# Tile 5's transposition moved from TensorE to memory moves and VectorE, in a fused linear-attention and MLP kernel

## The chip, the core and the metric

The kernel runs on one core of a Trainium2 chip. The core has a matrix engine (TensorE, "PE"; its weight loads are listed apart as "PEld"), VectorE ("DVE"), ScalarE ("ACT"), GpSimd ("POOL") and SyncE ("SP", which here issues nearly all DMAs). The engines run their own instruction streams in order and wait for each other through semaphores; DMA transfers run on 16 DMA engines of the core. The metric is the device time of one execution in microseconds (us). The kernel before took 416.17 us (median of three runs, 414.56 to 416.19).

## What is computed

An input `x` of 2048 tokens by 512 features is layer-normalised (no learned scale), and the result `xn` goes into two branches that are added to `x`:

```
xn  = (x - mean(x)) / sqrt(var(x) + 1e-5)
q, k, v = xn @ wqkv                    # 32 heads of 16
pq, pk  = phi(q), phi(k)               # phi(t) = t + 1 if t > 0 else exp(t), plus 1e-6
A   = (pq @ (pk^T v)) / (pq . sum(pk)) # per head
B   = relu(xn @ w1 + b1)^2 @ w2 + b2   # 1376 hidden units
out = x + A @ wo + B
```

All inputs and outputs are float32.

## The kernel before

The 2048 tokens are 16 tiles of 128 tokens. Products are made in a reduced float32 format on PE, in three passes of a high and a low part (`h` and `l`): high x high, high x low, low x high. So each operand is first split: the high part is a rounding copy (ACT mostly), the low part the difference (DVE or POOL).

The first part of the program, about the first 100 us, is the one that matters here. It goes over the 16 tiles, normalises each, brings it in two layouts and forms the key side of the attention:

- `xp[i]` is the normalised tile with tokens on partitions. Split by `tokens(i)` (L349: high on ACT, low on POOL) it is one operand of `kx(i)`.
- The same tile with features on partitions ("turned") is split into the column slots of `xsb` (`xs0` or `xs1`, chosen by `cols(i)`): `high` on ACT (L325), `low` on DVE (L328). `project(i, ...)` (L367, twelve matmuls) multiplies it with the key weights into a PSUM bank `pk{i}`. The first eight matmuls need the high part, the last four the low part.
- `phi_k` (L380) makes `phi` of it: two activations on ACT (L361, L363), one instruction on DVE (L365, tile `k`). `parts(i)` (L373) splits that: high on ACT (L377), low on DVE (L378, tile `pk`).
- `kx(i)` (L384, twelve matmuls) adds the products of tile i's tokens and its `pk` to four PSUM banks.

The loop at L779 runs i from 2 to 15. Its pass i issues, in this order: the memory moves that are due (`move()`, L784), `project(i)`, the transposes of a later tile, `phi_k(i)`, the normalisation of a later group (`normalise(*soon)`), `parts(i)`, the token split of tile i + 1, the turn of tile i + 2 (L831, where that is done by DVE), statistics of a later tile, in passes 3 and 6 two stores of 1 MB each (`xsd`, L843 to 845), and last `kx(i - 1)`. The order of the program is the order on each engine, since the schedule is written by hand.

There are two ways to turn a tile.

- Tiles below `NDVE` (6 before the change, so tiles 0 to 5): `turned_pe` (L304) has four PE transposes against an identity (L309) into a PSUM bank; `high` and `low` read that bank, and `keep_t` copies it with ACT to SBUF so that SP can store it to `xTd` for later use (L337). Tiles 3, 4 and 5 are turned so in passes 2, 3 and 4, between `project(i)` and `kx(i - 1)` on PE.
- The other tiles go in pairs: `regroup` (L278) stores the pair of normalised tiles to a DRAM buffer `via` with one DMA (L282) and notes four moves that bring it back regrouped by blocks of 32 partitions into `xg` (L290). `move()` issues noted moves at the head of the next pass. Each move waits until the `via` store has landed. `turn` (L292, L294) is then one DVE instruction that transposes 32x32 blocks. No PE and no PSUM bank is used. For such tiles `xp[i]` is stored with its features regrouped.

Tiles 6 and 7 are the only ones below `NPE` = 8 that go the second way. Tiles below 8 are normalised by DVE (L269), later ones by ACT (L259).

Statistics (L230, L231) are gathered in groups that share two small activations and three small DVE instructions. The groups before the change:

```
soon = group(4, 6, 7)         # L628; measured before the loop, normalised in pass 2
if i == 2:                    # L834
    ahead[3] = statistics(5)  # normalised in pass 3
```

Tiles 8 and 9, 10 and 11, and so on follow in pairs (`ahead[4]`, `ahead[6]`, ...), normalised in passes 4, 6, 8 and 10. The pairs' moves are issued in passes 5, 7, 9 and 11, and their first tile is turned at the end of passes 6 and 8, then, from pass 11 on, in front of `phi_k`. The pair 6 and 7 is normalised in pass 2, moved at the head of pass 3 and turned at the end of passes 4 and 5.

In pass 3, before the moves, SP also loads the bias `b1` with four small DMAs (L780 to 783); it is first used after 100 us.

After the loop come the attention matrices and two rounds of the MLP and query products; the change doesn't touch them.

Of the kernel before, what the change touches and what calls it, by code (L numbers as in the profile page):

```python
# [7 lines left out]
F32 = mybir.dt.float32  # L8
# [5 lines left out]
P = 128  # L14
# [4 lines left out]
def kernel(  # L19
# [36 lines left out]
    NJ = D // P  # L56
    TB = 4
# [1 line left out]
    BT = TB * P  # L59
    NF = -(-F // P)  # L60
    NPE = 2 * TB
    NDVE = NPE - 2
    WARM = 11
    NP = NF // 2
    FP = NF * P
# [7 lines left out]
    work = ctx.enter_context(tc.tile_pool(name="work", bufs=1))  # L73
# [4 lines left out]
    def bank(name, tag="ps"):  # L78
        return psum.tile([P, 512], F32, name=name, tag=tag)

    def w512(name, tag, bufs):
        return work.tile([P, 512], F32, name=name, tag=tag, bufs=bufs)
# [8 lines left out]
    def two(name):  # L91
        return keep.tile([P, 2, 512], F32, name=name, tag=next_tag("x"))

    def four(name, tag, dt=F32, pool=None):
        return (pool or work).tile([P, TB, 512], dt, name=name, tag=tag)
# [7 lines left out]
    def gjc(ap):  # L103

        return ap.rearrange("p (j g c) -> p g j c", j=NJ, g=NJ)
# [11 lines left out]
    def split(h, l, src, eh, el):  # L117
        copy(eh, h, src)
        ENG[el].tensor_tensor(out=l, in0=src, in1=f32(h), op=OP.subtract)  # L119
# [35 lines left out]
    xr, xp, xg, tok, pk, kp = {}, {}, {}, {}, {}, {}  # L155
# [17 lines left out]
    def units(f):  # L173


        if f < NF - 1:
            return [(0, f * P, P)]
        return [(0, f * P + Q, 2 * Q), (2 * Q, f * P, Q), (3 * Q, f * P, Q)]
# [44 lines left out]
    def group(*tiles):  # L223
        return tiles, *(small.tile([P, 3, k], F32, name=f"{n}{tiles[0]}", tag=n) for n, k in (("st", 6), ("mv", 2), ("y", 3)))

    def measure(g, *ks):

        tiles, st, mv, _ = g
        for k in ks or range(len(tiles)):
            nc.vector.bn_stats(st[:, k, :], xr[tiles[k]])  # L230
            nc.vector.bn_aggr(mv[:, k, :], st[:, k, :])  # L231

    def statistics(*tiles):
        g = group(*tiles)
        measure(g)
        return g

    def roots(tiles, st, mv, y):

        n = len(tiles)  # L240
        nc.scalar.activation(y[:, 1, :n], mv[:, :n, 1], AF.Ln, bias=eps)
        nc.scalar.activation(y[:, 0, :n], y[:, 1, :n], AF.Exp, scale=-0.5)

    def normalise(tiles, st, mv, y):
# [18 lines left out]
        for k, i in enumerate(tiles):  # L263
            o, src = xp[i], xr[i]
            if i >= NDVE:

# [20 lines left out]
    def move(n=8):  # L287
        for _ in range(n):
            if moves:
                nc.sync.dma_start(*moves.pop(0))  # L290
# [6 lines left out]
    def slot(i):  # L297
        return slice((i % TB) * P, (i % TB + 1) * P)
# [5 lines left out]
    def turned_pe(i, n=1):  # L304

        t = [bank(f"pt{i}{k}", "acc" if i < 3 else "ps")[:, :D // n] for k in range(n)]
        for j in range(NJ):
            k, at = divmod(j * P, D // n)
            nc.tensor.transpose(t[k][:, at:at + P], xp[i][:, j * P:(j + 1) * P], ident)  # L309
        ones(i)  # L310
        return [p.rearrange("p (j t) -> p j t", j=NJ // n) for p in t]

    def transposed(i, n=1):

        b, at = i // TB, slot(i)
        if i < NDVE:
            t = turned_pe(i, n)
# [12 lines left out]
        def keep_t():  # L330
            o = t[0]
            if i < NDVE:
                o = w512(f"t{i}", "p", 6).rearrange("p (j t) -> p j t", j=NJ)
# [11 lines left out]
    def ones(i):  # L345

        nc.gpsimd.memset(xp[i][:, D - 1:] if i < NDVE else xp[i][:, NJ - 1, P - 1:], 1.0)

    def tokens(i):  # L349
        tok[i] = pair(f"tok{i}")  # L350
        h, l = tok[i][:, 0], tok[i][:, 1]
        src = xp[i]
        if i >= NDVE:
            h, l, src = gjc(h), gjc(l), src.rearrange("p g (j c) -> p g j c", j=NJ)
        split(h, l, src, "act", "pool")
        if NDVE <= i + 1 < NT:
            ones(i + 1)
# [9 lines left out]
    def project(i, ps, w, steps, first=True, last=True):  # L367

        for n, (j, u, v) in enumerate(steps):
            nc.tensor.matmul(ps, lhsT=cols(i)[u][:, j, slot(i)], rhs=w[v][:, j, :], start=first and n == 0,  # L370
                             stop=last and n == len(steps) - 1)

    def parts(i):  # L373

        p = kp[i]
        pk[i] = pair(f"pk{i}")
        copy("act", pk[i][:, 0], p, 1e-6)  # L377
        nc.vector.scalar_tensor_tensor(pk[i][:, 1], p, 1e-6, f32(pk[i][:, 0]), op0=OP.add, op1=OP.subtract)  # L378

    def phi_k(i, ps, mid=lambda: None, late=lambda: None):  # L380
        kp[i] = w512(f"k{i}", "p", 6)
        phi(ps, kp[i], mid, late)
# [139 lines left out]
    t, rk = two("x0"), four("rk", "r0")  # L522
# [17 lines left out]
    groups = {}  # L540
    x4, x8 = four("x4", "r1"), four("x8", "r2")
    for i0 in range(0, NT, TB):
        a = first_xp[i0]
        for k in range(TB):
            xp[i0 + k] = a[:, k]
        if i0 + TB <= NDVE:
            continue
        n = TB if i0 >= NPE else NPE - NDVE
        o = work.tile([P, n, 512], F32, name=f"xg{i0}", tag="r0" if i0 + TB == NT else "r3" if i0 >= NPE else "rc")
        for k in range(0, n, 2):  # L550
            i = i0 + TB - n + k
            u, v = (t.rearrange("p a (g c) -> p (a g c)", g=NJ) for t in (a[:, TB - n + k:][:, :2], o[:, k:k + 2]))
            groups[i + 1] = [t.rearrange("p (g n) -> p g n", g=NJ) for t in (u, v)]
            u, v = (t.rearrange("p (g i c) -> p g i c", g=NJ, i=2) for t in (u, v))
            for m in range(2):
                xp[i + m], xg[i + m] = u[:, :, m], v[:, :, m]
# [68 lines left out]
    load_x(12, two("x12"))  # L625
    load_x(14, two("x14"))
    project(2, pks[2], wk, HL)
    soon = group(4, 6, 7)  # L628
    phi_k(0, pks[0])
    measure(soon, 0)  # L630
    tokens(0)
# [5 lines left out]
    measure(soon, 1)  # L637
    tokens(1)
    parts(1)
    measure(soon, 2)  # L640


    def tokens_sum(n, tag):
        return keep.tile([P, 2, 2, 512], F32R, name=f"T{n}", tag=tag)
# [32 lines left out]
    def fetch():  # L677
        while todo and len(held) < 3:
            held.append(todo.pop(0)())
# [89 lines left out]
    def more(i=None):  # L769

        if i is None or i > 12:
            do(extra, counts[0].pop(0))


    ahead = {}
# [1 line left out]
    kxp = [bank(f"kx{c}", "acc") for c in range(NJ)]  # L777
    kx(0)
    for i in range(2, NT):  # L779
        if i == 3:  # L780
            nc.sync.dma_start(b1s[:, :NF - 1], b1[:(NF - 1) * P].rearrange("(f p) -> p f", p=P))
            for a, o, n in units(NF - 1):
                nc.sync.dma_start(b1s[a:a + n, NF - 1:], b1[o:o + n, None])
        move()  # L784
        fetch()
        ps = pks[i] if i < 3 else bank(f"pk{i}")
        if i > 2:
            project(i, ps, wk, HL)
        high = low = keep_t = lambda: None
        if i + 1 < NDVE:  # L790
            high, low, keep_t = transposed(i + 1)

        soon_turned = transposed(i + 2) if 11 <= i and i + 2 < NT else ()

        def mid():
            high()
            more(i)

        def late():
            if soon:  # L800
                roots(*soon)
            low()
            more(i)

        if i == 12:
            rawz = raw_1(NF - 1)
            T.update({n: tokens_sum(n, f"B{n - 1}") for n in (1, 2)})
        if i == 12:
            w = load_1("q", 0)
        if i == 13:  # L810
            todo_1 = operands_first(0, w)
            extra.append(todo_1.pop(1))
        if i == 14:
            z = pair("w1z0")
            extra.append(lambda: split(z[:, 0], z[:, 1], rawz, "act", "dve"))
            o34 = halves(four("Tf", "r0"))
            extra.extend(sums_of(xT[NB - 1], xT[NB - 2], *o34))
            lows = [extra.pop() for k in range(2)]
            extra += [todo_1[0], lows[1], todo_1[1], lows[0], *todo_1[2:]]
        phi_k(i, ps, mid, late)  # L820
        more(i)
        run(*soon_turned)
        later = normalise(*soon) if soon else []
        parts(i)
        keep_t()
        if i == 2:
            tokens(2)
        if i + 1 < NT:
            tokens(i + 1)
        run(*later)  # L830
        if NDVE <= i + 2 < 13:  # L831
            run(*transposed(i + 2))
        pieces([3, 1, 1, 2, 1][i - 11] if i > 10 else 0)
        if i == 2:  # L834
            ahead[3] = statistics(5)
        if i + 2 in (4, 6, 8, 10):
            ahead[i + 2] = group(i + 6, i + 7)
        if i < 10:
            measure(ahead[(i + 2) // 2 * 2], i % 2)
        soon = ahead.get(i + 1, ())  # L840
        if i in (3, 6):

            b = i // 6  # L843
            for u in range(2):
                nc.sync.dma_start(xsd[b][u], f32(cols(b * TB)[u]))
        kx(i - 1)
        more(i)
# [53 lines left out]
    for n in range(2):  # L901
        t1, t2 = NB - 1 - 2 * n, NB - 2 - 2 * n
        x1, x2 = xsb
        tag = "acc" if n else "ps"
# [299 lines left out]
        f = NF - 2  # L1204
# [36 lines left out]
        for e, f in enumerate(waiting[:-2]):  # L1241
# [3 lines left out]
            if e:  # L1245
                do(w2next, 2)
                if e + 8 < NF:
                    g = waiting[e + 8]
# [77 lines left out]
```

## Time and profile before

| | before |
|---|---|
| median of three runs | 416.17 us (414.56, 416.17, 416.19) |
| profiled execution, span from first to last instruction | 412.7 us |
| profiled execution, its own time | not listed beside the span; the three runs lie 1.9 to 3.5 us above the span |
| PE busy | 407.9 us (99%), 1835 matmuls |
| DVE, ACT, POOL busy | 314.5, 270.4, 50.1 us |
| mean granted PE clock | 1.000 |
| DMA | 54.62 MB, mean 132 GB/s |

In the views below a row of a timeline has the start in us, the length in us, the engine, the line of the kernel, the operation and its tiles; in brackets stands the idle time before it and what ended it. "SPq" rows are DMA issues: the length is that of the issue on SP, not of the transfer. The DMA view has the number of DMAs, their size and the median time from issue to landing. The chain of waits has start, length and what ran. In a tile's name the buffer number is left out, so `xs0h` is the high part of all tiles in that buffer and `pk` stands both for the PSUM banks and for the split result.

### The profile page before, as it was taken

What the parts mean: (1) busy time and instruction counts of PE and PEld (TensorE: products, weight loads), DVE (VectorE), ACT (ScalarE), POOL (GpSimd) and SP (SyncE); (2) the same over time, 40 slices, a digit from 0 to 9 for tenths busy, and PEclk for the clock granted to TensorE, in tenths of its full rate; (3) what the DMA queues carried; (4) which work ended last, traced back from release to release, by engine and by line L of the source; (5) the groups of instructions that cost most, each with busy time, mean ns of one, the idle gap of its engine ahead of it and who ended that gap; (6) DMA issues with size and microseconds to landing.
All of it is one profiled execution on the core that took longest, in us unless ns stands there. A gap on an engine that the chain in (4) does not pass through costs nothing.

```text
span 412.7 us, 5426 instructions
## 1 busy us (share of the span) xinstructions
PE 407.9 (99%) x1835; PEld 337.4 (82%) x1835; DVE 314.5 (76%) x584; ACT 270.4 (66%) x487; POOL 50.1 (12%) x70
## 2 busy tenths in 40 slices
PE   8999999999999999999999999999999999999996
PEld 7788888888888888888878888888888888878885
DVE  6895667797899898998439996468989685449843
ACT  5867767756678789788547631567588857737420
POOL 3241222220320000020000040100000200000310
PEclk9999999999999999999999999999999999999999
DMA  7879572810422322273267992421120881024502
GB/s 230 297 238 356 205 229 102 252 30 2 116 64 58 96 56 69 81 195 61 110 238 245 380 198 77 127 52 51 53 78 25 229 187 43 2 89 166 103 0 102
DMA packets 44925, 54.62 MB, mean 132 GB/s; under 512 B 7905, under 2 KB 29153, under 8 KB 43618
## 3 DMA queue, kind: packets, MB, share of 16 engines
q1 hardware_dynamic: 42594, 50.09, 36.9%
q0 software_dynamic: 2304, 4.20, 6.3%
q8 instruction: 14, 0.23, 0.2%
q14 instruction: 13, 0.11, 0.1%
HBM read 41.16 MB, written 13.11 MB: 131 GB/s over the span
## 4 chain that ended last, share of the span: by engine, by line
PE 98%; DVE 1%; DMA 1%; ACT 0%; issue 0%
PE acc L130 37%; PE b L489 32%; PE pk L370 11%; PE kx L390 11%; PE acc L500 2%; PE pz L130 1%; PE pkv L877 1%; PE pm L130 1%; PE pz0b L130 1%; PE b L130 1%; PE pt L309 1%; DMA x<-in_A_x_dram 1%; PE acc L507 0%; DVE st L230 0%; PE end L130 0%; DVE xp L269 0%
## 5 line engine op out<-in xcount | busy, mean ns | idle before, releaser
L130 PE MATMUL acc<-w2r,s 128*128 128x512 f32 x477 | 112.8, 390 | 0.0
L130 PEld LDWEIGHTS acc<-w2r,s 128*128 128x128 f32 x477 | 89.4, 188 | 19.2 <-issue 0.7
L489 PE MATMUL b<-T,aop 128*128 128x512 f32 x336 | 83.4, 389 | 0.0
L489 PEld LDWEIGHTS b<-T,aop 128*128 128x128 f32 x336 | 63.1, 188 | 13.1
L390 PE MATMUL kx<-pk,tok 128*128 128x512 f32 x192 | 46.5, 391 | 0.0
L390 PEld LDWEIGHTS kx<-pk,tok 128*128 128x128 f32 x192 | 35.8, 188 | 7.7 <-ACT pk L111 0.2
L489 PE MATMUL b<-xs0h,aop 128*128 128x512 f32 x112 | 36.9, 390 | 0.0
L1007 POOL DMA_DIRECT2D res<-in_B_b_dram x16 | 14.1, 1069 | 182.7 <-DVE dt L431 64.3
L130 PE MATMUL acc<-mh,aTsr 128*128 128x512 f32 x112 | 35.6, 389 | 0.0
L1015 DVE TENSOR_TENSOR res<-acc,res 128x512 f32<-128x512 f32 x16 | 11.0, 692 | 23.1 <-PE acc L130 18.5
L119 POOL TENSOR_TENSOR tok<-xp,tok 128x512 fp32r<-128x512 f32 x16 | 21.7, 1358 | 55.4 <-ACT tok L111 55.4
L122 DVE TENSOR_TENSOR w2r<-r,w2r 128x512 fp32r<-128x512 f32 (+2 forms) x35 | 25.2, 722 | 0.1
L111 ACT ACTIVATE aop<-S 128x512 fp32r<-128x512 f32 x28 | 17.5, 624 | 11.0 <-DVE S L706 11.0
L130 PEld LDWEIGHTS acc<-mh,aTsr 128*128 128x128 f32 x112 | 21.0, 188 | 4.4
L489 PEld LDWEIGHTS b<-xs0h,aop 128*128 128x128 f32 x112 | 21.0, 188 | 4.3
L119 DVE TENSOR_TENSOR aop<-S,aop 128x512 fp32r<-128x512 f32 x28 | 19.5, 698 | 4.8 <-ACT aop L111 4.4
L119 DVE TENSOR_TENSOR s<-c,s 128x512 fp32r<-128x512 f32 x20 | 13.6, 689 | 11.5 <-ACT s L111 11.4
L130 PE MATMUL acc<-ml,aTsr 128*128 128x512 f32 x56 | 21.8, 389 | 0.0
L489 PE MATMUL b<-xs0l,aop 128*128 128x512 f32 x56 | 21.8, 389 | 0.0
L111 ACT ACTIVATE w2r<-r 128x512 fp32r<-128x512 f32 x32 | 19.6, 619 | 2.6 <-DMA out_dram<-res 2.0
L111 ACT ACTIVATE T<-Tf 128x512 fp32r<-128x512 f32 x16 | 9.5, 627 | 16.4 <-DVE Tf L649 16.3
L489 PE MATMUL b<-xs1h,aop 128*128 128x512 f32 x56 | 19.5, 389 | 0.0
(197 smaller groups left out, 770.9 us busy)
## 6 DMA issues: line engine op xcount, KB each, us to landing
r<-in_B_w_dram SPq DMA_DIRECT2D x49, 256.0 KB, 3.0
res<-in_A_x_dram SPq DMA_DIRECT2D x8, 512.0 KB, 4.7
res<-in_B_b_dram POOLq DMA_DIRECT2D x16, 256.0 KB, 5.8
out_dram<-res SPq DMA_DIRECT2D x15, 256.0 KB, 2.1
x<-in_A_x_dram SPq DMA_DIRECT2D x5, 512.0 KB, 6.0
via<-xp SPq DMA_DIRECT2D x5, 512.0 KB, 2.7
xg<-via SPq DMA_DIRECT2D x20, 128.0 KB, 2.9
xTd<-t SPq DMA_DIRECT2D x8, 256.0 KB, 3.2
```

Of the source, the lines that this page charges most:

```text
L111: nc.scalar.activation(o, i, AF.Copy, bias=bias)
L119: ENG[el].tensor_tensor(out=l, in0=src, in1=f32(h), op=OP.subtract)
L122: nc.vector.tensor_tensor(out=l, in0=src, in1=f32(h), op=OP.subtract)
L130: nc.tensor.matmul(ps, lhsT=a[u], rhs=b[v], start=first and n == 0, stop=last and n == 2)
L309: nc.tensor.transpose(t[k][:, at:at + P], xp[i][:, j * P:(j + 1) * P], ident)
L370: nc.tensor.matmul(ps, lhsT=cols(i)[u][:, j, slot(i)], rhs=w[v][:, j, :], start=first and n == 0, stop=last and n == len(steps) - 1)
L390: nc.tensor.matmul(kxp[c], lhsT=tok[i][:, u, c * P:(c + 1) * P], rhs=pk[i][:, v], start=i == 0 and (u, v) == first, stop=i == NT - 1 and ( ...
L489: nc.tensor.matmul(ps, lhsT=a[u][:, j * P:(j + 1) * P], rhs=b[v][:, j, :], start=first and j == 0 and n == 0, stop=last and j == 1 and n == 2,
L500: nc.tensor.matmul(ps, lhsT=s[u][:, k * P:(k + 1) * P], rhs=w2s[NF - 1][u][:, a:z], start=first and u == 0, stop=stop and u == 1)
L877: nc.tensor.matmul(ps[:, at], lhsT=wvs[:, c, at], rhs=kxs[c // 2][:, c % 2, at], start=c == 0 and j == 0, stop=c == NJ - 1 and j == NJ - 1 ...
L1007: nc.gpsimd.dma_start(r[:, i], b2[None, :].partition_broadcast(P), accum_op=OP.add)
L1015: nc.vector.tensor_tensor(out=r[:, a:z], in0=ps, in1=r[:, a:z], op=OP.add)
```

## The change

`NDVE` becomes 5, so tile 5 is turned the second way, alone: it gets its own `xg` buffer (one tile wide) and its own `via` store and four moves. Its four PE transposes, its PSUM bank and its copy out of PSUM go. The statistics groups become 4 and 5 (before the loop, normalised in pass 2) and 6 and 7 (measured at the end of pass 2, normalised in pass 3, where tile 5 was). Tile 5's moves are issued at the head of pass 3, those of tiles 6 and 7 at the head of pass 4. Tile 5 is turned by DVE in pass 4, in front of `phi_k(4)`; tiles 6 and 7 at the end of passes 4 and 5, as before. The loads of `b1` are issued in pass 5 instead of pass 3, still ahead of that pass's moves.

```diff
-    NDVE = NPE - 2
+    NDVE = NPE - 3
...
-        n = TB if i0 >= NPE else NPE - NDVE
+        n = TB if i0 >= NPE else TB // 2
+        if i0 < NPE:
+            i = i0 + TB - n - 1
+            one = work.tile([P, 512], F32, name=f"xg{i}", tag="r0")
+            xp[i], xg[i] = (t.rearrange("p (g n) -> p g n", g=NJ) for t in (xp[i], one))
+            groups[i] = [xp[i], xg[i]]
...
-    soon = group(4, 6, 7)
+    soon = group(4, 5)
...
-    measure(soon, 2)
...
-        if i == 3:
+        if i == 5:
             nc.sync.dma_start(b1s[:, :NF - 1], b1[:(NF - 1) * P].rearrange("(f p) -> p f", p=P))
...
-        if i + 1 < NDVE:
+        if i < NDVE:
             high, low, keep_t = transposed(i + 1)
...
-        if NDVE <= i + 2 < 13:
+        if NDVE < i + 2 < 13:
             run(*transposed(i + 2))
...
         if i == 2:
-            ahead[3] = statistics(5)
+            ahead[3] = statistics(6, 7)
```

## The prediction

> **What bounds the kernel now.** I read the page's busy shares and clock first, then its chain of waits, then each engine's instructions in order of time between 12 and 100 us. From the page:
>
> ```profile
> PE 407.9 (99%) x1835; PEld 337.4 (82%) x1835; DVE 314.5 (76%) x584; ACT 270.4 (66%) x487; POOL 50.1 (12%) x70
> PEclk9999999999999999999999999999999999999999
> ...
> PE 98%; DVE 1%; DMA 1%; ACT 0%; issue 0%
> ```
>
> TensorE (PE) works without a pause at full granted clock and is 98% of the chain. So a microsecond taken from PE is a microsecond of the kernel, and a microsecond in which PE has nothing to do is lost for good, because nothing behind it has slack to give it back. Two questions decide: how much PE work goes, and whether the operands that now come another way still arrive ahead of PE. The chain, around the place of the change (start, length):
>
> ```profile
> 31.63 0.44 PE pt L309 x4
> ```
>
> and PE's instructions there (start, length; a row of x12 starts 2.72 us before its successor):
>
> ```profile
> 31.82 3.02 PE L390 MATMUL kx<-pk,tok 128*128 128x512 f32 x12
> ...
> 34.67 0.39 PE L370 MATMUL pk<-wkh,xs0h 128*128 128x512 f32 x1
> ...
> 40.11 0.39 PE L370 MATMUL pk<-wkh,xs0h 128*128 128x512 f32 x1
> ...
> 42.83 2.88 PE L390 MATMUL kx<-pk,tok 128*128 128x512 f32 x12
> ```
>
> The `pt` row of the chain is tile 5's turn. 34.67 and 40.11 are the projections of tiles 5 and 6, 42.83 the sums of tile 5. After its start, the stretch in which PE paused most is this one (length; busy time of PE, PEld, DVE, ACT, POOL; granted clock, DMA share, GB/s):
>
> ```profile
> 6.00:8.00 2.00, 1.37 (x8) 1.08 (x9) 1.84 (x7) 1.54 (x3) 0.22 (x2) 1.00 1.02 356
> ```
>
> **The change, part by part.** I name a pass of the loop by its i: pass i projects tile i.
>
> *Removed.* Four PE transposes (0.44 us by the chain) and tile 5's copy out of PSUM on ACT (off the chain, as ACT is 66% busy). Everything on PE behind them can come 0.44 us sooner: **-0.44**.
>
> *Statistics.* Tile 5 is measured with tile 4, tiles 6 and 7 two at a time one pass later. The number of measurements is the same. VectorE (DVE) in passes 1 to 3, and the DMA issues of SyncE (SP):
>
> ```profile
> 20.89 0.68 DVE L230 BATCH_NORM_STATS2 st<-x 128x6 f32<-128x512 f32 x1
> ...
> 23.46 1.46 DVE L269 TENSOR_SCALAR xp<-x,mv,y 128x512 f32<-128x512 f32 x3
> ...
> 28.80 0.55 DVE L269 TENSOR_SCALAR xp<-x,mv,y 128x512 f32<-128x512 f32 x1
> ```
>
> ```profile
> 24.95 0.33 SPq L282 DMA_DIRECT2D via<-xp  x1
> ...
> 25.95 0.75 SPq L781 DMA_DIRECT2D b1s<-in_B_b_dram  x1
> 26.76 1.87 SPq L783 DMA_DIRECT2D b1s<-in_B_b_dram  x3
> 28.73 1.79 SPq L290 DMA_DIRECT2D xg<-via  x4
> 30.62 0.53 SPq L337 DMA_DIRECT2D xTd<-t  x1
> 31.19 0.62 SPq L845 DMA_DIRECT2D xsd0h<-xs1h  x1
> 31.86 0.46 SPq L845 DMA_DIRECT2D xsd0l<-xs1l  x1
> ```
>
> Before, the three normalisations at 23.46 are tiles 4, 6, 7, and right behind them, at 24.95, tiles 6 and 7 leave for memory; their four moves back (28.73) go out ahead of the two 1 MB stores of pass 3 (31.19, 31.86). Now 4 and 5 come at about 22.7 (the measurement at 20.89, with what follows it 0.8 us, is gone ahead of them), and 6 and 7 take the place that tile 5 had at 28.80. The second ends at 28.80 + 0.46 + 0.55 = 29.8, and the pair leaves for memory then: **4.85 us later**, straight ahead of the two stores. Its moves back wait for that to land and so are issued behind the stores. That is the step to price.
>
> *Tiles 6 and 7.* DVE in passes 4 to 6; the transposes are those of tiles 6, 7 and 8:
>
> ```profile
> 32.78 0.69 DVE L328 TENSOR_TENSOR xs0l<-pt,xs0h 128x512 fp32r<-128x512 f32 x1 [2.02 <-ACT xs0h L325]
> ...
> 35.38 0.70 DVE L294 STREAM_TRANSPOSE t<-xg 128x512 f32<-128x512 f32 x1
> ...
> 41.16 0.70 DVE L294 STREAM_TRANSPOSE t<-xg 128x512 f32<-128x512 f32 x1
> ...
> 46.38 0.70 DVE L294 STREAM_TRANSPOSE xT<-xg 128x512 f32<-128x512 f32 x1
> ```
>
> Nothing in the old trace shows the new way of tiles 6 and 7, but pass 6 has the same sequence of issues for tiles 10 and 11. Ahead of it in this list are the moves of tiles 8 and 9, which have no stores before them:
>
> ```profile
> 40.81 1.74 SPq L290 DMA_DIRECT2D xg<-via  x4
> ...
> 47.65 0.34 SPq L282 DMA_DIRECT2D via<-xp  x1
> 48.03 0.43 SPq L845 DMA_DIRECT2D xsd1h<-xs0h  x1
> 48.55 0.74 SPq L845 DMA_DIRECT2D xsd1l<-xs0l  x1
> 50.39 3.91 SPq L290 DMA_DIRECT2D xg<-via  x4
> ```
>
> The DMA view of 50 to 56 us gives the time from issue to landing of the four moves at 50.39 (median, last column), that of 40.8 to 42.6 us the same for tiles 8 and 9:
>
> ```profile
> xg<-via SPq DMA_DIRECT2D x4, 128.0 KB, 6.4
> ```
>
> ```profile
> xg<-via SPq DMA_DIRECT2D x4, 128.0 KB, 2.8
> ```
>
> and DVE shows what it did to tile 10:
>
> ```profile
> 58.82 0.71 DVE L294 STREAM_TRANSPOSE xT<-xg 128x512 f32<-128x512 f32 x1 [1.47 <-DMA xg<-via]
> 60.23 0.69 DVE L328 TENSOR_TENSOR xs1l<-xT,xs1h 128x512 fp32r<-128x512 f32 x1 [0.70 <-ACT xs1h L325]
> ```
>
> From leaving to the transpose it was 58.82 - 47.65 = 11.17 us. Tile 10 could afford that: its moves go out a pass later, and two passes lie between leaving and its use. Tile 6 leaves in pass 3 and is turned at the end of pass 4. At 29.8 + 11.17 its transpose starts at **41.0** instead of 35.38. The bounds: with moves that land like those of tiles 8 and 9 (2.74 for the way out as from 47.65 to 50.39, 1.3 to the last issue, 2.8 to land) 36.7; with the 256 KB store of tile 4 (the row at 30.62), which now also stands between, at the 356 GB/s of the busy stretch above (0.7 us), 41.7. I take 41.0, since the sequence matches that row.
>
> PE is free for tile 6 at 40.11 - 0.44 = 39.67. Transpose to finished copy took 1.41 us (58.82 to 60.23), so the first matmul can start at 42.4: **+2.75**. Behind the waiting transpose on DVE stand the low part of tile 6, a measurement and pass 5's `k` and `pk`; on ACT the copy and pass 5's two activations; on SP the store of tile 6, the four b1 loads (2.6 us of issue, moved here from pass 3, where they stood in the shadow of a landing) and the moves of tiles 8 and 9.
>
> *What comes of that wait.* ACT in passes 4 to 6, and in pass 12:
>
> ```profile
> 37.05 0.62 ACT L325 ACTIVATE xs0h<-t 128x512 fp32r<-128x512 f32 x1
> ...
> 39.82 0.63 ACT L111 ACTIVATE pk<-k 128x512 fp32r<-128x512 f32 x1 [0.97 <-DVE k L365]
> ...
> 43.03 0.60 ACT L361 ACTIVATE k<-pk 128x512 f32<-128x512 f32 x1 [0.50 <-PE pk L370]
> ```
>
> ```profile
> 79.60 0.63 ACT L111 ACTIVATE pk<-k 128x512 fp32r<-128x512 f32 x1
> ```
>
> Tile 7's transpose stood 41.16 - 35.38 = 5.78 behind tile 6's, of which 0.95 was the copy at 37.05 coming late; that goes, so it now starts at 41.0 + 4.83 = 45.8. Pass 5's high part of `pk` ended 39.82 + 0.63 - 37.67 = 2.8 behind tile 6's copy, so now at 42.4 + 2.8 = 45.2, just when PE is through with tile 6 (42.4 + 2.72 = 45.1): **+0.1**. From 41.16 to 47.65 was 6.49, of which 0.50 was a wait for PE that goes too: tiles 10 and 11 leave at 45.8 + 6.0 = 51.8, **4.15 us later than before, while PE is only 2.4 late**. DVE, ACT and the landings are one chain there (copy, activations, `k`, `pk`, transpose, and so on), so 4.15 stays with it, and PE meets it twice:
>
> ```profile
> 61.87 0.39 PE L370 MATMUL pk<-wkh,xs1h 128*128 128x512 f32 x1
> ...
> 80.91 2.88 PE L390 MATMUL kx<-pk,tok 128*128 128x512 f32 x12
> ```
>
> Tile 10 was ready 1.64 us ahead of 61.87, and 4.15 - 2.4 - 1.64 gives **+0.1**. Tile 12's sums at 80.91 need the `pk` that ends at 79.60 + 0.63 = 80.23, behind a transpose that itself waited for moves; slack 0.68, and 4.15 - 2.5 - 0.68 gives **+0.95**. Tiles 8 and 9 have room: tile 6's transpose ends at 41.7, SP stores it (0.5), issues the b1 loads by 45.0 and the moves by 46.8; they land by 49.6, and tile 8's transpose, 46.38 + 4.15, is due at 50.5.
>
> *Tile 5's own way.* It leaves at about 23.8 and is half as large as a pair. With some 2.8 us to land, the moves' 1.8 to issue (the row at 28.73) and 2.8 for the last to land it is back at about 31. Its transpose is 0.70; pass 4 has DVE idle then, because the low part at 32.78 had to wait 2.02 us for its copy. So tile 5's way costs **0**. Without that cover (a landing after 32.8) tile 5's projection, due at 34.67 - 0.44, would wait as long as the landing is late. I do not expect that, and since PE waits for tile 6 later anyway, most of it would be the same wait.
>
> *Sum.* -0.44 + 2.75 + 0.1 + 0.1 + 0.95 = **+3.5 us**, on a span of 412.7, so 416.2. What lies outside the span, 3.5 us to the median of 416.17, I leave as it is: **419.7 us**.
>
> [...] PE would stand still for about 2.75 us. In the stretch of 6 to 8 us it paused 0.63 us in all, and the granted clock stayed 1.00; nothing longer is to be seen. [...]
>
> **The rivals.**
> A, hidden (ends the other way). The moves of tiles 6 and 7 land in 2.8 us, as those of tiles 8 and 9 did, in spite of the stores; tile 6 is turned at 36.7. It decides at 39.67 - 1.41 = 38.26: any transpose before that leaves PE without a pause, and only -0.44 remains: **415.7**. For it: the moves are four DMAs of 128 KB against 2 MB, and a fair share between them would do. Against it: the row with 6.4, in the same order of issue. [...]
> B, partly hidden. Landing between 38.3 and 39.7: **416 to 418**.
> C, the clock drops. The first twelve matmuls after the pause run at half speed, 5.44 instead of 2.72: **422.4**. For it only the length of the pause; against it that pauses of 0.63 us did nothing to the clock, and that this is one pause of 2.75.
> D, tile 5 itself comes late. Its pieces are 512 B instead of 1 KB. At 2 us late it moves tile 5's projection, but tile 6's wait then shrinks by the same: 419.7 to 420.5.
>
> **How the numbers follow.** Forecast and D together 0.66, A 0.14, B 0.09, C 0.11. A measurement of this kernel tells about 0.5% (2.1 us, the spread of the three runs) from no change. Under 414.1 only a faster mechanism that I do not see: 0.03 (from A). 414.1 to 418.25: A, B and a small tail of the forecast, 0.21. Above: 0.76. The forecast's own range, from 41.0 +/- 1 us, is 418.5 to 421. The range 415.6 to 421.8 takes in A and B and leaves out C.
>
> **What would show it.** Right: no `pt` row at 31; the pair of tiles 6 and 7 leaving at 29.8 and its moves issued at 32.5 with over 5 us to landing; DVE's second transpose at 40 to 42 with a wait on `xg<-via`; PE waiting some 2.7 us for ACT's `xs0h` at 39.7, and shorter waits at about 64 and 84; granted clock 1.00. Wrong: moves landing in 3 us; PE without pauses; a clock under 1.00 at 42 to 46.

## The result, and the profile after

| | before | after |
|---|---|---|
| runs | 6: 414.45 to 414.60 (three), 416.17 to 416.19 (three) | 6: 419.06 to 420.72 |
| median | 415.38 us (of the lower three 414.56) | 419.36 us |
| profiled execution: span | 412.7 us | 417.9 us |
| the same execution's own time | 414.4 us (see below) | 419.62 us |
| mean granted PE clock in it | 1.000 | 0.996 |
| PE busy | 407.9 us (99%) | 409.5 us (98%) |

The changed kernel takes 1.0116 times as long, 95% interval 1.0100 to 1.0132, about 4.8 us more. The runs of before lie in two groups; the ratio is taken against the lower one, which holds the profiled execution too: a later run of before had the same span of 412.7 us and a time of 414.38, and the profiled execution of after had 419.62 - 417.9 = 1.7 us outside its span. The spans differ by 5.2 us. At PE's last matmul the difference is 4.96 us (its end at 414.42 instead of 409.46); the rest comes behind it.

The page of after, its busy shares, the clock in 40 slices and the chain's shares by engine:

```profile
PE 409.5 (98%) x1831; PEld 338.2 (81%) x1831; DVE 315.5 (75%) x585; ACT 269.9 (65%) x486; POOL 49.0 (12%) x70
...
PEclk9999899999999999999999999999999999999999
...
PE 93%; DMA 3%; DVE 1%; SPq 1%; ACT 1%; issue 0%; DVEq 0%
```

Four PE instructions are gone (1831 instead of 1835), yet PE is busy for 1.6 us more, and one slice shows a lower clock. DMA, DVE, ACT and SP's issues now hold 6% of the chain (2% before). Where they entered it (start, length):

```profile
29.63 2.74 DMA via<-xp
...
32.39 0.74 SPq L290
...
33.17 1.24 SPq L290
...
34.45 1.27 SPq L290
...
35.77 5.69 DMA xg<-via
...
41.58 0.72 DVE t L294
...
42.33 0.64 ACT xs0h L325
...
43.01 4.61 PE pk L370 x12
47.62 2.73 PE kx L390 x12
...
82.98 2.72 PE pk L370 x12
...
85.72 2.98 PE kx L390 x12
```

Read from the top: tiles 6 and 7 leave at 29.63, their moves are issued one after the other from 32.39, the last one is under way for 5.69 us, and only then come DVE's transpose, ACT's copy and PE. The 43.01 row is tile 6's projection. Its twelve matmuls take 4.61 us to the end of the last one; those of the next passes take 2.72. From its first matmul to the first of the sums behind it are 47.41 - 43.01 = 4.40 us. The waits of PE give the pause ahead of it (total, times, longest):

```profile
PE pk L370 <- ACT xs0h L325: 3.3, 1, 3.3
```

The windows of 1 us around it (length; busy time of PE, PEld, DVE, ACT, POOL; granted clock, DMA share, GB/s):

```profile
42.00:43.00 1.00, 0.00 (x0) 0.00 (x0) 0.30 (x2) 0.67 (x2) 0.00 (x0) 1.00 0.44 176
43.00:44.00 1.00, 0.99 (x4) 0.86 (x5) 1.00 (x2) 0.97 (x2) 0.00 (x0) 1.00 0.51 154
44.00:45.00 1.00, 1.00 (x4) 0.77 (x4) 0.97 (x3) 0.11 (x1) 0.00 (x0) 0.53 0.59 110
45.00:46.00 1.00, 1.00 (x4) 0.81 (x3) 0.25 (x2) 0.85 (x2) 0.00 (x0) 0.50 0.58 4
46.00:47.00 1.00, 1.00 (x4) 0.71 (x4) 1.00 (x2) 0.30 (x1) 0.62 (x1) 0.50 0.27 73
47.00:48.00 1.00, 1.00 (x5) 0.82 (x4) 0.30 (x2) 0.78 (x2) 0.75 (x2) 0.76 0.88 287
```

PE does nothing in the first row, is granted full speed for about one more microsecond, and then half of it. The loss, 0.47 + 0.50 + 0.50 + 0.24 = 1.71 us of clock, is a half-speed stretch of 1.71 / 0.50 = 3.4 us.

SP's issues in the order in which they went out:

```profile
23.68 0.33 SPq L282 DMA_DIRECT2D via<-xp  x1
...
26.57 2.00 SPq L290 DMA_DIRECT2D xg<-via  x4
29.63 0.34 SPq L282 DMA_DIRECT2D via<-xp  x1
...
30.65 0.74 SPq L849 DMA_DIRECT2D xsd0h<-xs1h  x1
31.44 0.45 SPq L849 DMA_DIRECT2D xsd0l<-xs1l  x1
32.39 4.56 SPq L290 DMA_DIRECT2D xg<-via  x4
```

Tile 5 leaves at 23.68 and its moves go out at 26.57. The pair leaves at 29.63; two stores of 1 MB go out behind that, and the pair's moves behind those. Before, the moves (28.73) went ahead of the stores (31.19). The DMA views of 26.5 to 28.6 us and of 32 to 37 us have the median time to landing of tile 5's moves and of the pair's:

```profile
xg<-via SPq DMA_DIRECT2D x4, 64.0 KB, 2.2
```

```profile
xg<-via SPq DMA_DIRECT2D x4, 128.0 KB, 6.7
```

And DVE's transposes of tiles 5, 6, 10 and 14, with the wait ahead of each in brackets:

```profile
31.02 0.71 DVE L294 STREAM_TRANSPOSE t<-xg 128x512 f32<-128x512 f32 x1
...
41.58 0.71 DVE L294 STREAM_TRANSPOSE t<-xg 128x512 f32<-128x512 f32 x1 [6.12 <-DMA xg<-via]
...
63.87 0.71 DVE L294 STREAM_TRANSPOSE xT<-xg 128x512 f32<-128x512 f32 x1 [1.90 <-DMA xg<-via]
...
83.61 0.71 DVE L294 STREAM_TRANSPOSE xT<-xg 128x512 f32<-128x512 f32 x1 [1.98 <-DMA xg<-via]
```

Tile 5, which the change is about, comes in time and costs nothing. Tile 6 is 6.2 us later than before (35.38), tile 10 5.05 (58.82).

### The profile page after: what moved, and what is told of

It is laid out like the page before. It is cut to its first block, busy times and chain, and to the rows that moved or that the text cites. A ratio compares the mean times of both kernels' runs of the same rounds, so it can differ in the third digit from the quotient of the medians.

```text
span 417.9 us, 5430 instructions
## 1 busy us (share of the span) xinstructions
PE 409.5 (98%) x1831; PEld 338.2 (81%) x1831; DVE 315.5 (75%) x585; ACT 269.9 (65%) x486; POOL 49.0 (12%) x70
## 4 chain that ended last, share of the span: by engine, by line
PE 93%; DMA 3%; DVE 1%; SPq 1%; ACT 1%; issue 0%; DVEq 0%
PE acc L130 36%; PE b L489 32%; PE pk L370 10%; PE kx L390 9%; PE acc L500 2%; DMA xg<-via 1%; PE pz L130 1%; PE pkv L881 1%; SPq L290 1%; PE pm L130 1%; DMA via<-xp 1%; PE pz0b L130 1%; PE b L130 1%; DMA x<-in_A_x_dram 1%; PE pt L309 0%
```

## The experiments

The theory: tiles 6 and 7 leave a pass later, and so their moves queue behind two 1 MB stores on SP's queue; that holds up tile 6, and the late chain of DVE, ACT and landings does the rest. The rivals: the loss comes from tile 5's own way or from the moved `b1` loads; or it comes from the clock.

**The stores behind the moves.** The changed kernel with one edit: the two stores are issued at the head of pass 4, right behind the moves of tiles 6 and 7.

```diff
         move()
+        if i == 4:
+            for u in range(2):
+                nc.sync.dma_start(xsd[0][u], f32(cols(0)[u]))
...
-        if i in (3, 6):
+        if i == 6:
```

> The changed kernel with one edit: the two 1 MB stores of pass 3 are issued at the head of pass 4, right behind the moves of tiles 6 and 7 instead of ahead of them. My theory (the moves stand in line behind 2 MB of stores): the moves land in about 2.8 us, tile 6 is transposed at about 36.6 instead of 41.58, PE has no pause at tile 6, the granted clock stays 1.00, and what is left is the 0.44 us of the four PE transposes: 415.0 us against 415.4 before, 4.4 us less than the changed kernel. Rival 1 (the loss comes from tile 5's own way, or from the pair leaving 4.7 us later whatever stands ahead of it): 418 to 419.4, with the pause still there.

Measured: 414.29 us (11 runs) beside 414.59 (17 runs of before), ratio 0.9995 (0.9983 to 1.0006), span 412.5, clock 1.000. SP's issues, the landing of the moves in the DMA view of 32 to 35 us, DVE's transpose of tile 6, and PE's first matmul of it:

```profile
32.56 1.73 SPq L290 DMA_DIRECT2D xg<-via  x4
34.34 0.43 SPq L791 DMA_DIRECT2D xsd0h<-xs1h  x1
34.81 0.43 SPq L791 DMA_DIRECT2D xsd0l<-xs1l  x1
```

```profile
xg<-via SPq DMA_DIRECT2D x4, 128.0 KB, 2.8
```

```profile
36.82 0.71 DVE L294 STREAM_TRANSPOSE t<-xg 128x512 f32<-128x512 f32 x1 [1.37 <-DMA xg<-via]
```

```profile
39.57 0.39 PE L370 MATMUL pk<-wkh,xs0h 128*128 128x512 f32 x1
```

The pair leaves just as late as in after, and its moves are issued at the same time, 32.56 against 32.39. But their issue takes 1.73 us instead of 4.56, they land in 2.8 us instead of 6.7, and PE starts tile 6 without a pause, 0.54 us ahead of before (40.11). The whole loss is gone with the order of two stores; tile 5's way and the `b1` loads, which are still in this kernel, cost PE nothing. What is issued behind the stores is slower now: the four `b1` loads take 4.90 us to issue (2.50 in after), the moves of tiles 8 and 9 go out behind them at 44.06, and DVE waits 1.69 us for these before tile 8's transpose. PE has room enough there and doesn't pause. What the removed PE transposes bring is seen on PE to the end (its last matmul ends 0.46 us sooner, at 409.00 instead of 409.46); in the time it is within the uncertainty.

**One store behind.** The same with only the second store moved, so 1 MB is ahead of the moves instead of 2 or 0.

```diff
         move()
+        if i == 4:
+            nc.sync.dma_start(xsd[0][1], f32(cols(0)[1]))
...
-            for u in range(2):
+            for u in range(2 if b else 1):
```

> The changed kernel with one of the two 1 MB stores behind the moves of tiles 6 and 7, the other ahead as before. My theory (time in line by bytes ahead): 1 MB at the 418 GB/s of that stretch is 2.5 us, so tile 6 is transposed at about 39.1, PE's pause is about 0.9 us, the clock stays 1.00, and the chain is 2.8 instead of 5.3 us late: about 417.4 us. Rival 3 (the moves wait for as long whatever the bytes ahead, as soon as one store is): 419.4. Rival 1 (tile 5's own way, not the stores): 419.4 too.

Measured: 416.01 us (415.33 to 416.73) beside 414.52, ratio 1.0034 (1.0018 to 1.0050), span 413.6, clock 1.000. The moves in the DMA view of 32 to 36 us, DVE's transpose and PE's first matmul of tile 6:

```profile
xg<-via SPq DMA_DIRECT2D x4, 128.0 KB, 4.4
```

```profile
38.56 0.71 DVE L294 STREAM_TRANSPOSE t<-xg 128x512 f32<-128x512 f32 x1 [3.14 <-DMA xg<-via]
```

```profile
39.99 0.50 PE L370 MATMUL pk<-wkh,xs0h 128*128 128x512 f32 x1 [0.28 <-ACT xs0h L325]
```

| bytes of stores ahead of the moves | 0 | 1 MB | 2 MB |
|---|---|---|---|
| issue of the four moves on SP | 1.73 us | 2.68 us | 4.56 us |
| median landing | 2.8 us | 4.4 us | 6.7 us |
| tile 6 transposed | 36.82 | 38.56 | 41.58 |
| PE's pause at tile 6 | 0 | 0.28 us | 3.27 us |
| time | 414.29 us | 416.01 us | 419.36 us |

The landing grows with the bytes ahead, by 1.6 us for the first store and 2.3 us for the second. The time came out lower than forecast: the late chain met PE at tile 10 (0.45 us: tile 8's sums start 0.11 us later than in before, tile 9's, behind tile 10's projection, 0.56) but no more at tile 12, where tile 14's transpose at 78.96 was only 0.7 us later than in before. The lateness of that chain is not handed on in full; some of it is taken up by its waits.

**The groups alone.** Before, with only the statistics groups changed. Tile 5 stays on PE, and `b1` in pass 3.

```diff
-    soon = group(4, 6, 7)
+    soon = group(4, 5)
...
-    measure(soon, 2)
...
-            ahead[3] = statistics(5)
+            ahead[3] = statistics(6, 7)
```

> The kernel before with the groups of statistics alone changed (4 and 5, then 6 and 7); tile 5 is still turned by PE and the b1 loads stay in pass 3. My theory (the whole loss comes with the pair's later leaving, and the chain of VectorE, ScalarE and landings sets the end, not the sum of PE's pauses): 419.4 us, the same as the changed kernel, with PE's pause some 0.44 us shorter because PE still does the transposes in it. If PE's own sum set the end: 419.8. Rival 1 (tile 5's own way is needed for the loss): 415.4.

Measured: 419.81 us (419.12, 418.68, 420.49, 420.72), ratio 1.0122 (1.0098 to 1.0146), span of the profiled execution 417.4. PE's wait and DVE's transposes of tiles 6 and 14:

```profile
PE pk L370 <- ACT xs0h L325: 2.7, 1, 2.7
```

```profile
41.83 0.71 DVE L294 STREAM_TRANSPOSE t<-xg 128x512 f32<-128x512 f32 x1 [6.13 <-DMA xg<-via]
...
83.33 0.71 DVE L294 STREAM_TRANSPOSE xT<-xg 128x512 f32<-128x512 f32 x1 [1.55 <-DMA xg<-via]
```

The groups alone bring the whole loss, without tile 5's new way. In this profiled execution the clock was 1.000 throughout, in spite of a pause of 2.7 us; at 420.49 and 420.72 us its mean was 0.991 and 0.996. Why it fell there and not here is open.

**The `b1` loads alone.** Before, with only the four loads moved to pass 5.

```diff
-        if i == 3:
+        if i == 5:
             nc.sync.dma_start(b1s[:, :NF - 1], b1[:(NF - 1) * P].rearrange("(f p) -> p f", p=P))
```

> The kernel before with the four b1 loads alone moved from pass 3 to pass 5, still ahead of that pass's moves. My theory: no change (415.4 us, span 412.7), the moves of tiles 8 and 9 are issued up to 2.6 us later and still land before their transpose at 46.4. Rival 4 (the b1 loads hold up a pair of moves that PE waits for): up to 2 us more and a pause of PE at tile 8.

Measured: 414.38 us in a single run beside 414.52, span 412.7, the same as before. The moves of tiles 8 and 9 were issued at 41.26 (40.81 before), and tile 8 was transposed at 46.24 without a wait. No effect is seen.

**The pause filled.** The changed kernel with twelve matmuls more ahead of `project(6)`, into the bank that the projection then overwrites, so that PE stands still for less time and the operands still come late.

```diff
         ps = pks[i] if i < 3 else bank(f"pk{i}")
+        if i == 6:
+            for _ in range(12):
+                nc.tensor.matmul(ps, lhsT=wk[0][:, 0, :P], rhs=wk[0][:, 0, :], start=True, stop=True)
```

> The changed kernel with twelve matmuls more (their result is overwritten) between the sums of tile 4 and the projection of tile 6, so in PE's pause; they take 2.72 us of the 3.3. My theory: the granted clock stays 1.00 and tile 6's projection takes 2.72 instead of 4.61 us, but the time stays at 419.4, because the chain of VectorE, ScalarE and landings behind tile 6's transpose is 5.3 us late by tile 14 and PE waits for it then (a pause of about 1.5 us before the sums of tile 12, some of it at tile 10). Rival 2 (PE's lost clock is a part of the time): 417.5.

Measured: 419.03 us (418.97 to 419.33), ratio 1.0106 (1.0090 to 1.0122), span 417.3, clock 0.999. PE's rows of the fill, of tile 6's first matmul and of the sums of tiles 5 and 12:

```profile
39.43 2.88 PE L793 MATMUL pk<-wkh 128*128 128x512 f32 x12
42.84 0.50 PE L370 MATMUL pk<-wkh,xs0h 128*128 128x512 f32 x1 [0.53 <-ACT xs0h L325]
...
45.69 2.97 PE L390 MATMUL kx<-pk,tok 128*128 128x512 f32 x12
...
85.12 3.01 PE L390 MATMUL kx<-pk,tok 128*128 128x512 f32 x12 [0.51 <-ACT pk L111]
```

The pause was 0.53 us and tile 6's projection ran at full speed: from 42.84 to the sums at 45.69 it is 2.85 us, in after 4.40. Yet the time is only 0.33 us lower than after's. PE, now 1.7 us further at 45.69 than in after (47.41), waits for the chain of DVE, ACT and landings at tile 10 and again at tile 12, where the sums start at 85.12, in after at 85.72. The lost clock of after lay almost wholly in time that PE would have spent waiting later.

**One group of four.** To let the pair leave early, as before the change, tiles 4 to 7 share one statistics group, whose small buffers are widened to four tiles, and are normalised in pass 2.

```diff
...
-    soon = group(4, 5)
+    soon = group(4, 5, 6, 7)
...
     parts(1)
+    measure(soon, 2, 3)
...
-            ahead[3] = statistics(6, 7)
+            pass
```

> The changed kernel with tiles 4, 5, 6 and 7 in one group of statistics: all four are normalised in pass 2, so the pair 6 and 7 leaves at about 26 instead of 29.63 and its moves are issued in pass 3 ahead of the stores, as they were before the change; tile 5 still goes through memory. My theory: no pause at tile 6, about 415.0 us (before less 0.44), at most 0.3 more where DVE's longer pass 2 shows. Rival 1 (tile 5's own way costs the time): about 419.

Measured: 416.33 us, ratio 1.0035 (1.0020 to 1.0050). Tile 6 was transposed at 39.27 without a wait for a DMA, as forecast, but the time is 1.3 us above the forecast. PE's sums of tile 2, and DVE and POOL in pass 2:

```profile
29.02 2.61 PE L390 MATMUL kx<-pk,tok 128*128 128x512 f32 x8 [1.76 <-DVE pk L378]
```

```profile
24.41 2.89 DVE L269 TENSOR_SCALAR xp<-x,mv,y 128x512 f32<-128x512 f32 x4
27.22 1.75 DVE L378 SCALAR_TENSOR_TENSOR pk<-k,pk 128x512 fp32r<-128x512 f32 x1
```

```profile
25.66 2.75 POOL L119 TENSOR_TENSOR tok<-xp,tok 128x512 fp32r<-128x512 f32 x2 [5.05 <-ACT tok L111]
```

PE waits 1.76 us for tile 2's `pk`. Its low part stands behind the normalisations on DVE, and both were slower than forecast: a normalisation took 2.89 / 4 = 0.72 us (1.46 / 3 = 0.49 before) and the low part 1.75 (0.69 in after), while POOL was splitting tokens. In the profiled execution (418.05 us) the clock fell to 0.50 after this pause of 1.76 us; in the other five (416.14 to 416.35) the mean clock was 0.999 to 1.000.

**The low part first.** The same group of four, with tile 2's split ahead of the normalisations.

```diff
...
+        if i == 2:
+            parts(i)
         later = normalise(*soon) if soon else []
-        parts(i)
+        if i > 2:
+            parts(i)
```

> The kernel with one group of four again, but in pass 2 the split of tile 2's result (which the sums of tile 2 need) is issued ahead of the four normalisations instead of behind them. In the run without this, PE waited 1.76 us for that split, which itself took 1.75 instead of 0.7 us while GpSimd split two tiles of tokens. My theory (DVE's long pass 2 was the whole of that loss; tile 5's way and the pair's early leaving cost nothing): no pause of PE at the sums of tile 2, pair 6 and 7 back before its transpose is due, 414.2 us against 414.6 before. Rival (DVE slowed by GpSimd is late for something else, or the eight moves in a row come late): 415 to 416.5.

Measured: 416.65 us, ratio 1.0046 (1.0033 to 1.0060), near the rival's 415 to 416.5 and not the theory's 414.2. PE's wait, and DVE and POOL in pass 2:

```profile
PE pt L309 <- DVE xp L269: 1.3, 1, 1.3
```

```profile
27.29 3.76 DVE L269 TENSOR_SCALAR xp<-x,mv,y 128x512 f32<-128x512 f32 x4
```

```profile
27.14 2.69 POOL L119 TENSOR_TENSOR tok<-xp,tok 128x512 fp32r<-128x512 f32 x2 [5.05 <-ACT tok L111]
```

The wait has moved from tile 2's `pk` to tile 4's normalised tile, and the normalisations, now beside POOL's work from their start until it ends at 29.83, take 3.76 / 4 = 0.94 us each. From 26.09 until they end at 31.05, DVE has no idle time. Neither place tried for the larger group brought a gain. Of the ways tried, only the order of the stores takes the loss away, and that version is not measurably different from before.

## Why the prediction was right

The forecast was 419.7 us and slower; measured were 419.36 us. The cause is the one that the prediction priced, and it is shown; that the time came out within 0.4 us is luck, as the sizes below tell. The loss goes with the stores' place, grows with their bytes, and comes with the groups alone. The sizes:

| step | forecast | measured in after |
|---|---|---|
| four PE transposes gone | -0.44 | -0.53 at tile 4's sums (36.86, before 37.39; 0.05 of it was there two passes earlier), -0.46 at the end of the kernel with the stores moved |
| tile 5 back and transposed | about 31, no wait | 31.02, no wait |
| pair 6 and 7 leaves; moves issued; landing | 29.8; 32.5; 6.4 us | 29.63; 32.39; 6.7 us |
| tile 6 transposed; first matmul | 41.0; 42.4 | 41.58; 43.01 |
| PE's pause at tile 6 | 2.75 us | 3.27 us |
| clock behind it | 1.00 | down to 0.50; tile 6's projection +1.89 us, of which 1.71 are clock by the windows above |
| chain of DVE, ACT and landings late at pair 10 and 11 | 4.15 (leaves 51.8) | 4.96 (leaves 52.61) |
| tile 5's sums, tile 10, tile 12's sums | +0.1, +0.1, +0.95 | 0, 0, +0.28 (with the clock kept: +0.13, +0.47, +0.79) |
| all, at PE's last matmul | +3.5 | +4.96 |
| outside the span | 3.5 us | 1.7 us |

The sum by the measured terms is -0.53 + 3.27 + 1.89 + 0.28 = +4.91, where tile 13's sums start (91.26, before 86.35). So the step is 1.4 us larger than forecast, and the time fits only because another number was off the other way: 3.5 us outside the span were taken from the median of the three runs shown, where a run has 1.7 us outside its own span (414.38 with a span of 412.7 before, 419.62 with 417.9 after). With that the forecast would have been 416.2 + 1.7 = 417.9. (The prediction also gives 2.1 us as the spread of the three runs; it is 416.19 - 414.56 = 1.63.)

Two terms of the sum were mis-sized, and the clock, which the sum left at 1.00, fell. One is the pause: the moves' issue stretched to 4.56 us (3.91 in the row that was taken as model) and the transpose came 0.6 us later than the model's, just under the upper bound of 41.7 that the prediction worked out with tile 4's store ahead of the moves. That points to this store as a term which the sum left out, though no run separates it. The other is how late the chain of DVE, ACT and landings ends, 4.96 us instead of 4.15 at the pair 10 and 11; the filled pause, where PE keeps its clock, ends +4.33 at tile 13's sums by that chain alone.

Of the rivals, A (hidden) is what the moves do when the stores are behind them: 2.8 us, 414.29. In the changed kernel, with 2 MB ahead, it was 6.7 us; the fair share that spoke for A was not seen. B is the kernel with one store ahead. D did not happen. C did: the clock fell, to the half speed that C supposed and that no row of before had shown (0.53, 0.50 and 0.50 from 44 to 47 us in after). The prediction had it at 0.11 and at +2.7 us, as a term of its own, and named a clock under 1.00 at 42 to 46 as a sign of being wrong. That sign came. The price given for it was too high: the 1.71 us of clock replaced most of the waits at tiles 10 and 12 that the prediction had summed up, and cost 0.33 us beyond them (419.36 against 419.03 with the pause filled). The two could not be added, because the later of two chains sets the end. For the same reason the wait forecast for about 64 did not come and the one at 84 was small.

How long a pause it takes, the runs do not tell. In after it was 3.27 us, and all six runs had a mean clock of 0.994 to 0.996; in the profiled execution of the group of four 1.76 us was enough (0.50 from 31 to 33 us). But 2.7 us did nothing in the profiled execution of the groups alone (1.00 in every window from 42 to 48 us), so the length of one pause does not decide. The start-up, ahead of all that the edits touch, says the same. Here are windows of 2 us from the profiled execution with the low part first:

```profile
4.00:6.00 2.00, 1.12 (x9) 0.93 (x8) 1.83 (x8) 0.99 (x4) 0.00 (x0) 1.00 0.94 311
6.00:8.00 2.00, 1.22 (x6) 0.85 (x7) 1.83 (x7) 1.42 (x3) 0.24 (x2) 0.89 1.02 369
8.00:10.00 2.00, 2.00 (x8) 1.72 (x7) 1.45 (x5) 1.45 (x5) 1.00 (x2) 0.50 0.62 185
```

PE paused for 1.66 us in all between 4 and 8 us, and the clock fell. In the profiled execution of the groups alone it was busy for 5.52 us between 0 and 8 us. If 3.15 of these lie in the first four, as in after, 2.37 are left for the next four, so it paused for 1.63 us there (an estimate); the clock stayed 1.00 up to 30 us. What else decides is open.

## What to carry to other kernels

When a producer is moved later, look at its DMA queue and not only at its engine: what is now issued ahead of its transfers, and how many bytes are that. Bulk stores that nobody waits for go behind the moves that the next tile waits for; here that order alone was worth 5 us (414.29 us instead of 419.36). All these transfers were issued on SP's queue; whether stores issued from another engine would hold the moves up as much was not tried. And do not add a lost clock to a late chain: a stall on one engine costs only what it exceeds the other chain's lateness by; here 1.71 us of clock cost 0.33 us.

## What the runs showed of the hardware

- Four 128 KB moves land in 2.8 us with no 1 MB store right ahead, 4.4 us behind a 1 MB store and 6.7 us behind two, issued on the same queue; the issues themselves take 1.73, 2.68 and 4.56 us of SP, and what stands behind them on SP is late as well (tile 5's store went out at 36.99 us in after, at 35.25 in before).
- In after the clock fell about 1 us after PE had started again, not during the pause: the windows show 1.00 at 43 to 44 us and 0.53 at 44 to 45.
- DVE's normalisation of a 128x512 tile took 0.49 to 0.50 us with POOL idle or nearly so (1.46 / 3 from 23.46 in before, 1.00 / 2 from 28.60 in after), and 0.72 and 0.94 where POOL's token splits ran beside it for over half of the time (from 24.41 in the group of four, from 27.29 with the low part first). The split of `pk` took 1.75 us in the group of four, from 27.22 to 28.97, with POOL splitting tokens until 28.41; but 0.69 in before, from 24.83 to 25.52, with POOL splitting tokens all the while (24.71 to 27.92). So POOL's work beside it did not always stretch it; what decides was not shown. The forecasts for the group of four had priced DVE's work as if it were alone.
